# Attention and GEGLU in one kernel: the q, k, v products as pairs of half-depth matmuls

## The chip, the cores and the metric

One Trainium2 chip, of which one core is used. The metric is the time of one execution in device microseconds (us), from runs on the chip; lower is better. The core's engines are TensorE (PE in the profile, its weight loads PEld), VectorE (DVE), ScalarE (ACT), GpSimd (POOL), and SyncE (SP), which here issues all transfers. Each takes its instructions in a fixed order. Matmul results go to PSUM, eight banks of 128 partitions x 512 float32, from where VectorE or ScalarE must fetch them.

## The reference

```python
def _A_ref(x, wqkv, wo):
    ...
    qkv = (lambda x, *d: x.transpose(*d))((x @ wqkv).reshape(B, S, 3, H, Dh), 2, 0, 3, 1, 4)
    q, k, v = qkv[0], qkv[1], qkv[2]
    scores = jnp.einsum("bhqd,bhkd->bhqk", q, k) * (Dh ** -0.5)
    p = _softmax(scores, axis=-1)
    o = jnp.einsum("bhqk,bhkd->bhqd", p, v)
    return (lambda x, *d: x.transpose(*d))(o, 0, 2, 1, 3).reshape(B, S, D) @ wo

def _B_ref(x, w_gate, w_up, w_down):
    return (_gelu(x @ w_gate) * (x @ w_up)) @ w_down

xn = _layernorm(x, axis=-1)
s = _A_ref(xn, A_wqkv, A_wo)
g = _silu(_B_ref(xn, B_w_gate, B_w_up, B_w_down))
return x + s * g
```

Here S = 2048 tokens, D = 576, 32 heads of 18, F = 4608; all float32. The change concerns `x @ wqkv` alone.

## The kernel before

The kernel has a first stage (the `pro` pool, up to line 384), in which x is normalised and transposed and q, k, v are computed and stored to DRAM; a long second stage, in which sections of the feed-forward part (gate, up, down) run interleaved with attention; and an epilogue. Everything that changes lies in the first stage.

**Precision.** A float32 operand is cut into a high part, rounded by the copy into an fp32r tile, and a low part, the difference. A product is the sum of high x high, low x high and high x low.

**Depth.** D = 576 is four tiles of 128 rows (KT = 4) and 64 rows over (HR = 64). A product's list `TERMS` has 12 full terms and two for the 64 rows over: there the x tile `xtr` holds the high part in partitions 0 to 63 and the low part in 64 to 127, and the weights' 64 rows are loaded twice, so that one matmul does both. That is 14 matmuls of 128 rows. `mm_terms` (L174) issues them into one PSUM tile `po`.

**Blocks.** Tokens are taken in four blocks of 512 (loop at L351). For each block nine q/k products (`project`, L286), each 128 columns of wqkv by 512 tokens, in the order 4, 5, 0, 1, 6, 7, 8, 2, 3; then `store_xt` (L245) stores the transposed x; then the 20 transposes of the next block (`transposes`, L234, five PSUM tiles `pt`, split into high and low parts by `split_t`, L185); then eight v products (`values_of`, L294), each 128 tokens by 288 columns. TensorE's order is the order of the program text; on the other engines a scheduler places each instruction, and SP's queue too.

**Evictions.** A q/k product is copied by ScalarE into a high part (L290), VectorE subtracts to the low part (L291), and both parts are stored (L293). The two tiles have three buffers each, so the fourth product waits for the first one's stores. A v product is copied by ScalarE (L300) into one of eight `vn` tiles and stored (L301).

**The next block's x.** `load_x` (L194) loads four tiles of 128 tokens (`xx`, four buffers, free again when the transposes of the block before have read them). `norm` (L203) takes statistics of each tile on VectorE (`bn_stats` L209, two per tile, `bn_aggr` L213), a square root on ScalarE (L215), small steps (L218 to L221), and normalises the four tiles (L223); ScalarE copies each tile's last 64 columns (L225). All of it is called in one piece after the fifth q/k product (n == 4, L370).

**Weights.** In block 0 the weights are loaded into five buffers `rawp` (L171) as they come free. The q/k weights are split on GpSimd (L106, L108), the v weights on ScalarE and VectorE (L116, L117). Eight small stores of zeros (L376) go to a DRAM tile `zq`.

**PSUM in this stage.** Three banks `po` and five banks `pt`.

Of the kernel before, what the change touches and what calls it, by code (L numbers as in the profile page):

```python
# [8 lines left out]
F32 = mybir.dt.float32  # L9
F32R = mybir.dt.float32r  # L10
AF = mybir.ActivationFunctionType
ALU = mybir.AluOpType
# [5 lines left out]
P = 128  # L18
NT = S // P
TB = 512  # L20
NB = S // TB
KT = 4
# [32 lines left out]
def f(ap):  # L55
    return ap.bitcast(F32)
# [13 lines left out]
def kernel(ctx: ExitStack, tc: tile.TileContext, x, wqkv, wo, w_gate, w_up, w_down, out):  # L70
# [65 lines left out]
    def load_xd(b, key=None):  # L136
# [13 lines left out]

    TERMS = [(0, k, 0) for k in range(KT)] + [(1, k, 0) for k in range(KT)] + [(0, k, 1) for k in range(KT)] \
        + [(0, KT, 2), (1, KT, 2)]

    FIRST_TERMS = sorted(TERMS[:2 * KT], key=lambda t: 2 * t[1] + 3 * t[0]) + TERMS[2 * KT:]


    with tc.tile_pool(name="pro", bufs=1) as pro, tc.tile_pool(name="pps", bufs=1, space=PSUM) as pps:
# [15 lines left out]

        def mm_terms(o, w, cols, xt, toks, swap=False, terms=TERMS):  # L174

            for i, (wp, k, xp) in enumerate(terms):
                xx = xt[xp][:, k, toks] if xp < 2 else xt[2][:, toks]
                ww = w[wp][:, k, cols] if k < KT else w[2 + wp]
                st, m = (xx, ww) if swap else (ww, xx)
                nc.tensor.matmul(o, st, m, start=(i == 0), stop=(i == len(terms) - 1))  # L180

        def tmp2(name):
            return pro.tile([P, TB], F32R, name=name, tag=name, bufs=3)

        def split_t(pt, k, xt):  # L185
# [16 lines left out]

        def norm(xr, b, between=None, behind=None):  # L203
            keep = tc.keep_in_program_order if b == 1 else lambda i: i
            st = pro.tile([P, 4, 8], F32, name="st", bufs=2)
            for j in range(4):
                bs = pro.tile([P, 2, 6], F32, name="bs", bufs=2)
                for h in range(2):
                    one = nc.vector.bn_stats(bs[:, h, :], xr[j][:, 288 * h:288 * h + 288])  # L209
                    keep(one)  # L210
                if behind and j == 0:
                    behind(one)
                nc.vector.bn_aggr(st[:, j, 0:2], bs)  # L213
            var, r, t = st[:, :, 1], st[:, :, 3], st[:, :, 4]
            nc.scalar.activation(t, var, AF.Sqrt, bias=eps)  # L215
# [12 lines left out]
        def warm(n):  # L228

            o = pps.tile([P, TB], F32, name="po", bufs=3)  # L230
# [21 lines left out]
        XT = [(pro.tile([P, KT, TB], F32R, name=f"xth{i}"), pro.tile([P, KT, TB], F32R, name=f"xtl{i}"),  # L252
               pro.tile([P, TB], F32R, name=f"xtr{i}")) for i in range(2)]
        VN = [pro.tile([P, H // 2, DH + 1], F32, name=f"vn{i}") for i in range(8)]
        eps = pro.tile([P, 1], F32, name="eps")
# [30 lines left out]
        def project(b, t, xt):  # L286
            o = pps.tile([P, TB], F32, name="po", bufs=3)
            mm_terms(o, WQK[t], slice(0, P), xt, all_t, terms=FIRST_TERMS if b == 0 and t == ORDER[0] else TERMS)
            hi, lo = tmp2("t1"), tmp2("t2")
            nc.scalar.activation(hi, o, AF.Copy)  # L290
            nc.vector.tensor_tensor(lo, o, f(hi), op=ALU.subtract)  # L291
            for i, a in enumerate((hi, lo)):
                nc.sync.dma_start(qk[i, t * P:(t + 1) * P, b * TB:(b + 1) * TB], f(a))  # L293

        def values_of(b, j, c, xt):
            t = b * 4 + j
            o = pps.tile([P, TB], F32, name="po", bufs=3)
            mm_terms(o[:, 0:D // 2], WV[c], slice(0, D // 2), xt, slice(j * P, (j + 1) * P), True)
            v = VN[2 * j + c]
            nc.scalar.activation(v[:, :, 1:DH + 1], o[:, 0:D // 2].rearrange("p (h d) -> p h d", d=DH), AF.Copy)  # L300
            nc.sync.dma_start(vs[t * P:(t + 1) * P, c * H // 2:(c + 1) * H // 2, :], v)  # L301

# [32 lines left out]
        xr = load_x(0)  # L335
        last = norm(xr, 0, first_hi, first_loads)
        raw, (raw_r, rest) = ahead_qk.pop(0)[1], ahead_qk.pop(1)
# [9 lines left out]
        for b in range(NB):  # L347
            for n, t in enumerate(ORDER):
# [693 lines left out]
```

## Time and profile before

| | us |
|---|---|
| median of 3 runs | 2547.48 (2546.96 to 2547.53) |
| profiled execution: span from first to last instruction | 2545.4 |
| first q/k matmul to first gate matmul | 11.68 to 196.27 |

The time of the profiled execution itself is not given apart from its span; the median of the runs is 2.1 us above that span. A row of a timeline is: start in us, length in us, engine, line, operation, tile written, tiles read, shape, count, and in brackets the idle time before it with what ended it. A row of groups is: line, engine, operation, tiles, shapes, count, then busy us, mean ns of one, and idle time before with what ended most of it. A row of the chain of waits has start, length, engine, tile and line. SPq is SP issuing a transfer; the transfer lands later.

### The profile page before, as it was taken

The page shows a single profiled execution, that of the slowest core. Times are in us where ns is not written, and L with a number is a line of the kernel's source. Part 1 is how long each engine was busy: PE and PEld are TensorE (multiplying, and loading weights), DVE is VectorE, ACT ScalarE, POOL GpSimd, SP SyncE. Part 2 cuts the span into 40 slices and gives each one's busy share as a digit, 9 for nine tenths or more (in the row PEclk, how much of TensorE's full clock was granted, in tenths as well). Part 3 has the DMA queues.
Part 4 walks back from the last instruction along what each step waited for, and adds up shares of the span by engine and source line. Part 5 has one row for each costly group of instructions (what it writes and reads, how often), then busy time and mean ns, then how long its engine had stood idle before and what let it go on. Part 6 is the DMA issues. An engine that isn't in the chain of part 4 may idle for free.

```text
span 2545.4 us, 63167 instructions
## 1 busy us (share of the span) xinstructions
PE 2538.4 (100%) x23974; PEld 2008.4 (79%) x23974; DVE 1950.4 (77%) x3499; ACT 1555.1 (61%) x3050; POOL 1320.7 (52%) x1447
## 2 busy tenths in 40 slices
PE   9999999999999999999999999999999999999999
PEld 8888877777777777777777787777777777787798
DVE  5316988888888888888888888888888888887277
ACT  3223366666677666676666677666676666676612
POOL 2117545555465554445565545554446555455675
PEclk9999999999999999999999999999999999999999
DMA  8876444444465444444455444444446444444483
GB/s 267 269 241 158 100 103 106 100 111 109 107 150 121 104 109 112 113 112 110 111 125 140 116 111 106 105 108 112 109 109 153 115 109 109 108 106 99 114 242 107
DMA packets 398686, 325.51 MB, mean 128 GB/s; under 512 B 117408, under 2 KB 309184, under 8 KB 398384
## 3 DMA queue, kind: packets, MB, share of 16 engines
q1 hardware_dynamic: 398384, 321.47, 49.7%
q8 instruction: 191, 3.13, 0.5%
q14 instruction: 111, 0.91, 0.1%
HBM read 266.63 MB, written 54.70 MB: 126 GB/s over the span
## 4 chain that ended last, share of the span: by engine, by line
PE 98%; ACT 1%; DVE 0%; DMA 0%; SPq 0%; issue 0%; ACTq 0%
PE pg L413 29%; PE py L465 18%; PE acc L764 18%; PE pm L698 9%; PE pe L729 9%; PE po L180 7%; PE pu L413 6%; PE po L902 2%; ACT pT L730 1%; PE pt L241 0%; SPq L665 0%; DMA xx<-in_A_x_dram 0%; DVE bs L209 0%; ACT t L426 0%; DMA KS<-qk 0%
## 5 line engine op out<-in xcount | busy, mean ns | idle before, releaser
L730 ACT ACTIVATE pT<-pe 128x512 f32<-128x512 f32 x2048 | 1153.3, 598 | 368.7 <-PE pm L698 226.3
L699 DVE TENSOR_REDUCE mx<-pm 128x1 f32<-128x512 f32 x2048 | 1249.6, 680 | 151.3 <-PE pm L698 149.0
L413 PE MATMUL pg<-xd,wh 64*128 64x512 f32 x2592 | 928.9, 390 | 0.0
L413 PE MATMUL pu<-xd,wh 64*128 64x512 f32 x2592 | 928.6, 390 | 0.0
L698 PE MATMUL pm<-KS,q 64*128 64x512 f32 x2048 | 779.0, 388 | 0.8 <-DMA KS<-qk 0.5
L729 PE MATMUL pe<-q,KS 64*128 64x512 f32 x2048 | 775.2, 387 | 0.0
L413 PEld LDWEIGHTS pg<-xd,wh 64*128 64x128 f32 x2592 | 476.5, 184 | 115.9 <-POOL wh L106 21.1
L413 PE MATMUL pg<-xd,wl 64*128 64x512 f32 x1296 | 501.6, 387 | 0.0
L413 PE MATMUL pu<-xd,wl 64*128 64x512 f32 x1296 | 501.4, 387 | 0.0
L413 PEld LDWEIGHTS pu<-xd,wh 64*128 64x128 f32 x2592 | 477.0, 184 | 2.0
L764 PE MATMUL acc<-pT,VS 128*32 128x512 f32 x4096 | 452.8, 594 | 0.0
L108 POOL TENSOR_TENSOR wl<-raw,wh 128x384 fp32r<-128x384 f32 x432 | 434.2, 1019 | 13.7
L106 POOL TENSOR_SCALAR hh<-t 128x512 fp32r<-128x512 f32 x128 | 79.1, 618 | 652.0 <-DVE t L440 637.8
L698 PEld LDWEIGHTS pm<-KS,q 64*128 64x128 f32 x2048 | 374.2, 184 | 31.1 <-DVE mx L699 4.3
L729 PEld LDWEIGHTS pe<-q,KS 64*128 64x128 f32 x2048 | 370.9, 184 | 21.9
L465 PE MATMUL py<-dh,hh 64*128 64x288 f32 (+1 forms) x2160 | 360.3, 294 | 0.3
L465 PE MATMUL py<-dl,hh 64*128 64x288 f32 (+1 forms) x2160 | 358.7, 292 | 0.0
L465 PE MATMUL py<-dh,hl 64*128 64x288 f32 (+1 forms) x2160 | 358.3, 292 | 0.0
L764 PEld LDWEIGHTS acc<-pT,VS 128*32 128x32 f32 x4096 | 127.4, 110 | 289.9 <-issue 278.0
L106 POOL TENSOR_SCALAR wh<-raw 128x384 fp32r<-128x384 f32 x432 | 217.2, 515 | 143.7 <-PE pu L413 83.4
L453 DVE TENSOR_TENSOR Y<-py,Y 128x288 f32<-128x288 f32 x544 | 227.1, 452 | 59.8 <-PE py L465 52.7
L413 PEld LDWEIGHTS pg<-xd,wl 64*128 64x128 f32 x1296 | 238.7, 184 | 32.1
(119 smaller groups left out, 3106.7 us busy)
## 6 DMA issues: line engine op xcount, KB each, us to landing
KS<-qk SPq DMA_DIRECT2D x1536, 36.0 KB
raw<-in_B_w_gate_dram SPq DMA_DIRECT2D x144, 288.0 KB
raw<-in_B_w_up_dram SPq DMA_DIRECT2D x144, 288.0 KB
raw<-in_B_w_down_dram SPq DMA_DIRECT2D x67, 576.0 KB
VS<-vs SPq DMA_DIRECT2D x128, 152.0 KB
qk<-t SPq DMA_DIRECT2D x72, 256.0 KB
q<-qk SPq DMA_DIRECT2D x384, 36.0 KB
xx<-in_A_x_dram SPq DMA_DIRECT2D x32, 288.0 KB
```

Source lines behind the costliest of these rows:

```text
L106: first = nc.gpsimd.tensor_scalar(hi, raw, 1.0, 1.0, op0=ALU.mult, op1=ALU.mult)
L108: low_part[:] = [keep(nc.gpsimd.tensor_tensor(lo, raw, f(hi), op=ALU.subtract))]
L180: nc.tensor.matmul(o, st, m, start=(i == 0), stop=(i == len(terms) - 1))
L413: nc.tensor.matmul(o, w[1 + wp][k][rr, c, :], xd[xp][k][rr, c, :], start=(i == 0), stop=(i == len(terms) - 1))
L453: one = kept(nc.vector.tensor_tensor(yy, py, yy, op=ALU.add))
L465: return nc.tensor.matmul(py, hs[g][a][rr, j * P:(j + 1) * P], wd[w][rr, g, 288 * c:288 * c + 288], start=start, stop=stop)
L698: nc.tensor.matmul(pm, QS[u, r][rr, t * P:(t + 1) * P], KS[(u * NA + c) % KB][r][rr, :], start=True, stop=True)
L699: nc.vector.tensor_reduce(MX[u][:, 2 * r + a, t, c:c + 1], pm, axis=AX.X, op=ALU.max)
L729: nc.tensor.matmul(pe, KS[(u * NA + c) % KB][r][rr, t * P:(t + 1) * P], QS[u, r][rr, :], start=True, stop=True)
L730: nc.scalar.activation(PT[u, kt][:, 2 * r + a, :], pe, AF.Exp, scale=SCALE)
L764: nc.tensor.matmul(ACC[u][32 * a:32 * a + 32, :], VS[(u * NA + c) % VB][:, v:v + 32], pt[:, a, :], start=first, stop=last, skip_group_chec ...
L902: nc.tensor.matmul(po, parts_of(b, j)[x_][:, k, :], OW[w][c][k], start=(i == 0), stop=(i == len(OUT) - 1))
```

## The change

Every product is now done in two halves of 64 rows, one in partitions 0 to 63, one in 64 to 127, each with its own PSUM tile; their matmuls are issued alternately. `REST` gives the halves the terms of the 64 rows over: one half gets two of the three, the other one, and which is which changes from product to product, so that a product has 27 halves. Where one half has one more, it waits in the list `HALVES` and is paired with the next product's first. A second x tile `xtq` holds the 64 rows with the high and low parts the other way round.

The two sums are added when a product is fetched: for q and k, ScalarE copies the first sum into the low part's tile, VectorE adds the second to it, ScalarE makes the high part, VectorE the low part; for v, ScalarE copies and VectorE adds. All PSUM tiles of the stage, the transposes' too, come from one pool of eight banks. `vn` has five tiles instead of eight. `norm` is cut in two functions: statistics of tiles 0 and 1 after one product, of tiles 2 and 3 after the next, and the rest after the one behind that (after products 5, 6 and 7 in block 0, after 3, 4 and 5 in later blocks).

```diff
-    TERMS = [(0, k, 0) for k in range(KT)] + [(1, k, 0) for k in range(KT)] + [(0, k, 1) for k in range(KT)] \
-        + [(0, KT, 2), (1, KT, 2)]
+    TERMS = [(0, k, 0) for k in range(KT)] + [(1, k, 0) for k in range(KT)] + [(0, k, 1) for k in range(KT)]
...
+    REST = [[[(0, KT, 2), (1, KT, 2)], [(0, KT, 2)]], [[(0, KT, 3)], [(0, KT, 3), (1, KT, 3)]]]
...
-        def mm_terms(o, w, cols, xt, toks, swap=False, terms=TERMS):
...
+        HALVES = [[], []]
+        PRODUCTS = [0]
+
+        def product(shape, operands, put, terms=TERMS):
+
+            pos = [pps.tile([P, TB], F32, name="po", bufs=8)[:, 0:shape] for _ in range(2)]
+            parity = PRODUCTS[0] % 2
+            PRODUCTS[0] += 1
+            left = [0]
+            for a in range(2):
+                mine = terms + REST[parity][a]
+                left[0] += len(mine)
+                for i, term in enumerate(mine):
+                    def step(a=a, i=i, term=term, n=len(mine)):
+                        st, m = operands(slice(HR * a, HR * a + HR), *term)
+                        nc.tensor.matmul(pos[a], st, m, start=(i == 0), stop=(i == n - 1))
+                        left[0] -= 1
+                        if left[0] == 0:
+                            put(*pos)
+                    HALVES[a].append(step)
+            while all(HALVES):
+                for half in HALVES:
+                    half.pop(0)()
...
-                nc.scalar.activation(xt[2], pt, AF.Copy)
-                nc.vector.tensor_tensor(xt[2][HR:P, :], pt[HR:P], f(xt[2])[HR:P, :], op=ALU.subtract)
+                for i, (hi, lo) in enumerate((HALF, HALF[::-1])):
+                    nc.scalar.activation(xt[2 + i], pt, AF.Copy)
+                    nc.vector.tensor_tensor(xt[2 + i][lo, :], pt[lo], f(xt[2 + i])[lo, :], op=ALU.subtract)
...
-            pts = [pps.tile([P, TB], F32, name="pt", bufs=KT + 1) for k in range(KT + 1)]
+            pts = [pps.tile([P, TB], F32, name="po", bufs=8) for k in range(KT + 1)]
...
-        VN = [pro.tile([P, H // 2, DH + 1], F32, name=f"vn{i}") for i in range(8)]
+        VN = [pro.tile([P, H // 2, DH + 1], F32, name=f"vn{i}") for i in range(5)]
...
+            def put(o, o2):
+                hi, lo = tmp2("t1"), tmp2("t2")
+                both = f(lo)
+                nc.scalar.activation(both, o, AF.Copy)
+                nc.vector.tensor_tensor(both, both, o2, op=ALU.add)
+                nc.scalar.activation(hi, both, AF.Copy)
+                nc.vector.tensor_tensor(lo, both, f(hi), op=ALU.subtract)
+                for i, a in enumerate((hi, lo)):
+                    nc.sync.dma_start(qk[i, t * P:(t + 1) * P, b * TB:(b + 1) * TB], f(a))
...
+            def put(o, o2):
+                vv = v[:, :, 1:DH + 1]
+                nc.scalar.activation(vv, o.rearrange("p (h d) -> p h d", d=DH), AF.Copy)
+                nc.vector.tensor_tensor(vv, vv, o2.rearrange("p (h d) -> p h d", d=DH), op=ALU.add)
+                nc.sync.dma_start(vs[t * P:(t + 1) * P, c * H // 2:(c + 1) * H // 2, :], v)
...
-                if n == 4 and b + 1 < NB:
-                    norm(xr, b + 1)
+                early = 0 if b == 0 else 2
+                if n in (4 - early, 5 - early) and b + 1 < NB:
+                    if n == 4 - early:
+                        st = pro.tile([P, 4, 8], F32, name="st", bufs=2)
+                    h = n - 4 + early
+                    norm_stats(xr, b + 1, st, range(2 * h, 2 * h + 2))
+                if n == 6 - early and b + 1 < NB:
+                    norm_rest(xr, st)
...
+        last_steps()
```

More of the change, by code (lines that the diff above doesn't have):

```diff
@@ L172, in load_rows, with last_steps, x_part, w_part @@
             return raw
-        def mm_terms(o, w, cols, xt, toks, swap=False, terms=TERMS):
[L176 to L180, printed above, removed]
+        HALVES = [[], []]
[19 more added lines that the diff above has]
+                    half.pop(0)()
+        def last_steps():
+            for half in HALVES:
+                while half:
+                    half.pop(0)()
+        def x_part(xt, rr, k, xp, toks):
+            return xt[xp][rr, k, toks] if xp < 2 else xt[xp][rr, toks]
+        def w_part(w, rr, k, wp, cols):
+            return w[wp][rr, k, cols] if k < KT else w[2 + wp][rr]
         def tmp2(name):
             return pro.tile([P, TB], F32R, name=name, tag=name, bufs=3)
+        HALF = slice(0, HR), slice(HR, P)
         def split_t(pt, k, xt):
@@ L201, in load_x, with norm_stats @@
             return xr
-        def norm(xr, b, between=None, behind=None):
+        def norm_stats(xr, b, st, js, behind=None):
             keep = tc.keep_in_program_order if b == 1 else lambda i: i
-            st = pro.tile([P, 4, 8], F32, name="st", bufs=2)
-            for j in range(4):
+            for j in js:
                 bs = pro.tile([P, 2, 6], F32, name="bs", bufs=2)
@@ L252 @@
         XT = [(pro.tile([P, KT, TB], F32R, name=f"xth{i}"), pro.tile([P, KT, TB], F32R, name=f"xtl{i}"),
[L253 to L254 removed]
+               pro.tile([P, TB], F32R, name=f"xtr{i}"), pro.tile([P, TB], F32R, name=f"xtq{i}")) for i in range(2)]
+        VN = [pro.tile([P, H // 2, DH + 1], F32, name=f"vn{i}") for i in range(5)]
         eps = pro.tile([P, 1], F32, name="eps")
@@ L335 @@
         xr = load_x(0)
-        last = norm(xr, 0, first_hi, first_loads)
+        st = pro.tile([P, 4, 8], F32, name="st", bufs=2)
+        norm_stats(xr, 0, st, range(4), first_loads)
+        last = norm_rest(xr, st, first_hi)
         raw, (raw_r, rest) = ahead_qk.pop(0)[1], ahead_qk.pop(1)
```

23 lines of the change are left out of this document (10 added, 13 removed).

## The prediction

> **What bounds the kernel now.** I read the page first, then the chain of waits in order of time, then the engines one by one over the first 100 us.
>
> ```profile
> span 2545.4 us, 63167 instructions
> PE 2538.4 (100%) x23974; PEld 2008.4 (79%) x23974; DVE 1950.4 (77%) x3499; ACT 1555.1 (61%) x3050; POOL 1320.7 (52%) x1447
> PE 98%; ACT 1%; DVE 0%; DMA 0%; SPq 0%; issue 0%; ACTq 0%
> ```
>
> TensorE ends the chain for 98% of the span, so time taken off it counts in full, and so does every wait put in front of it. In order of time, the part that changes is this:
>
> ```profile
> 11.68 30.17 PE po L180 x126
> 41.85 2.18 PE pt L241 x20
> 44.04 44.32 PE po L180 x238
> 137.04 59.23 PE po L180 x350
> 196.27 0.43 PE pg L413
> ```
>
> From 11.68 to 196.27 us TensorE never pauses: nine q/k products (126 = 9 x 14 matmuls), 20 transposes, eight v products and the nine of the next block (238 = 17 x 14), and so on. I call the products of a block P0 to P8 and v0 to v7. After 196.27 us the order of instructions is the same in both programs on every engine, so what is won or lost by then stays to the end.
>
> **The matmuls: what the pairs save.**
>
> ```profile
> 18.82 1.09 PE L180 MATMUL po<-xth,qh 128*128 128x512 f32 x4
> 22.09 1.09 PE L180 MATMUL po<-xth,qh 128*128 128x512 f32 x4
> 205.67 0.39 PE L413 MATMUL pg<-xd,wh 64*128 64x512 f32 x1
> 207.71 0.39 PE L413 MATMUL pg<-xd,wh 64*128 64x512 f32 x1
> 444.36 6.36 PE py L465 x95
> L465 PE MATMUL py<-dh,hh x32: 285/290/297, 444.2 to 450.2; 64*128 64x288 f32 x32
> ```
>
> One q/k product of 14 full matmuls takes 22.09 - 18.82 = 3.27 us (233.6 ns each). The gate and up products are already such pairs of halves: nine of them in 207.71 - 205.67 = 2.04 us, 226.7 ns a pair. The new product has 27 halves, 13.5 pairs: 3.06 us. 36 products save 36 x 0.21 = 7.6 us. A v product takes (44.32 - 9 x 3.27)/8 = 1.86 us, 132.9 ns a matmul; the down products' 48 pairs of 288 columns (three groups of 32 halves) take 6.36 us, 132.5 ns a pair, so 13.5 pairs take 1.79 us, and 32 products save 2.3 us. Together **-9.9 us**, and v gains only by the half pair that is gone.
>
> ```profile
> 238.11 0.39 PE L413 MATMUL pu<-xd,wh 64*128 64x512 f32 x1
> 238.43 0.40 PE L465 MATMUL py<-dh,hh 128*128 128x288 f32 x1
> 241.66 0.29 PE L465 MATMUL py<-dh,hl 128*128 128x288 f32 x1
> 241.88 0.50 PE L413 MATMUL pg<-xd,wh 64*128 64x512 f32 x1
> 242.22 0.39 PE L413 MATMUL pg<-xd,wl 64*128 64x512 f32 x1
> ```
>
> Going from pairs to full matmuls costs 0.32 - 0.23 = 0.09 us, the way back (0.22 - 0.13) + (0.34 - 0.23) = 0.2 us. The change goes out for transposes three times and back four times and loses the one switch at 196.27; without the two that fall into the pause of block 0 below that is **+0.6 us**. [...] If each of the five were a whole matmul record of 0.39 us, the sum would be 2.0 instead of 0.6 us; the rows above show less.
>
> **The evictions: what the sum costs.**
>
> ```profile
> L290 ACT ACTIVATE t<-po 128x512 fp32r<-128x512 f32 x36 | 21.4, 596 | 77.8 <-PE po L180 65.3 <-DMA qk<-t 9.6 <-issue 2.5
> L291 DVE TENSOR_TENSOR t<-po,t 128x512 fp32r<-128x512 f32 x36 | 24.9, 691 | 86.0 <-ACT t L290 76.7 <-DMA qk<-t 6.7 <-DMA raw<-in_A_wo_dram 2.6
> L437 ACT ACTIVATE t<-t 128x512 f32<-128x512 f32 x4 | 2.5, 632 | 1.2 <-DVE t L427 1.2
> L300 ACT ACTIVATE vn<-po 128x288 f32<-128x288 f32 x32 | 13.2, 418 | 40.0 <-PE po L180 40.0
> L209 DVE BATCH_NORM_STATS2 bs<-xx 128x6 f32<-128x288 f32 x32 | 12.8, 441 | 18.1 <-DMA xx<-in_A_x_dram 18.0
> L453 DVE TENSOR_TENSOR Y<-py,Y 128x288 f32<-128x288 f32 x544 | 227.1, 452 | 59.8 <-PE py L465 52.7
> ```
>
> A q/k product was two operations, 0.60 + 0.69; now it is copy, add, high part, low part: 0.60 + 0.69 + 0.63 (the nearest copy from SBUF is L437's) + 0.69 = 2.6 us one after the other. For the new SBUF-only subtraction the rows give 0.69 to 1.0 us (L117 below); I take 0.69. Within a q/k stage this is 1.4 us of VectorE per 3.06 us of TensorE and hidden: the eight banks hold four products. A v product was one copy on ScalarE; now it also needs an add on VectorE (0.45 us, L453's), **behind whatever VectorE has in its queue**, and there stand the next block's statistics, which waited 18 us for x without harm to anyone. The transposes' five banks, separate before, now come out of the same eight. The third copy of the remaining x rows (0.63 on ScalarE, 0.69 on VectorE per block) is in the chains below; three fewer fills of the v tiles gain nothing, as VectorE waits for x then anyway.
>
> ```profile
> 20.24 3.62 SPq L376 DMA_DIRECT2D zq<-ident  x8
> 23.96 1.82 SPq L293 DMA_DIRECT2D qk<-t  x4
> 32.56 1.15 SPq L171 DMA_DIRECT2D rawp<-in_A_wqkv_dram  x2
> 46.66 0.42 SPq L249 DMA_DIRECT2D xhs<-xth  x1
> 55.63 0.90 SPq L199 DMA_DIRECT2D xx<-in_A_x_dram  x2
> 20.37 2.53 POOL L108 TENSOR_TENSOR ql<-rawp,qh 128x512 fp32r<-128x512 f32 x2
> 26.41 0.60 ACT L290 ACTIVATE t<-po 128x512 fp32r<-128x512 f32 x1 [3.52 <-DMA qk<-t]
> 40.39 0.69 ACT L116 ACTIVATE vh<-rawp 128x576 fp32r<-128x576 f32 x1 [1.35 <-DMA rawp<-in_A_wqkv_dram]
> 40.98 0.24 ACT L225 ACTIVATE xx<-xx 128x64 f32<-128x64 f32 x1
> 28.14 1.01 DVE L117 TENSOR_TENSOR rest<-raw,rest 128x576 fp32r<-128x576 f32 x1
> 41.99 1.42 DVE L117 TENSOR_TENSOR vl<-rawp,vh 128x576 fp32r<-128x576 f32 x2
> 38.02 0.21 DVE L213 BATCH_NORM_AGGREGATE st<-bs 128x2 f32<-128x12 f32 x1
> 39.42 2.05 DVE L223 TENSOR_SCALAR xx<-xx,st 128x576 f32<-128x576 f32 x4
> 58.88 0.82 DVE L209 BATCH_NORM_STATS2 bs<-xx 128x6 f32<-128x288 f32 x2 [9.50 <-DMA xx<-in_A_x_dram]
> ```
>
> **Block 0, up to the transposes.** In the changed program's order SP has two v weight loads (the x2 at 32.56) ahead of the eight small stores (20.24) and the first q/k store. The second of them needs a buffer that GpSimd frees with its fifth low part, about 22.9 (20.37 + 2.53). So the first store goes at 22.9 + 0.5 + 3.6 = 27.1 instead of 23.96. P3's copy waits for P0's low part to be stored: that is the second store, 27.6, and 2.45 us to land (23.96 to 26.41) gives 30.0. From there ScalarE and VectorE run in one chain: P3 to 32.6, a weight split to 33.5, two tiles' statistics (2 x 1.03) to 35.6, P4's and P5's add, high and low parts to 39.6, the other two tiles' statistics to 41.7, square root and small steps (38.23 to 39.42, 1.2) to 42.9, first normalised tile at 43.4. TensorE arrives at 11.68 + 30.17 - 9 x 0.21 = 40.0. Then it needs five of the eight banks: two that P5 used, free by then, both of P6's, and the first of P7's. P7's copy stands on ScalarE behind the last normalised tile (44.9), that tile's 0.24 copy, two v weight splits (1.4), P6's high part (0.63) and itself takes 0.60: free at 47.8. Sixteen transposes (1.7) end at 49.5, where without waits it would be 42.15: **+7.4 us**. Bounds: 0, if stores and evictions run as early as before, and 10, with each SBUF subtraction at 1.0 us and the stores a microsecond later.
>
> **Block 0, v products.** v0 needs the first bank that the transposes fill. ScalarE first ends P7's high part and the last two v weight splits (1.4), then copies that bank (0.60), VectorE subtracts (0.69): free at 52.6, 3.1 us late. Before v0's add VectorE has seven more operations of 0.69 (three splits, two for the remaining rows, P8's add and low part), so it ends at 57.9; then come the statistics of block 2. Their x loads stand behind 2.36 MB of stores of transposed x. Before, from the first of these (46.66) to the first x in place (58.88) 3.43 MB took 12.2 us, 281 GB/s; now 2.65 MB from about 50.8 give 60.3, then one tile every 1.05 us, the fourth (issued behind v0's store) near 65. VectorE's order is three tiles, v1's add (64.0), the fourth tile, root, v2's add (67.2), four normalisations, v3's add (70.6). v5, v6 and v7 need the banks of v1, v2 and v3: v5 starts at 64.0, v6 at 67.2, v7 at 70.6 and ends at 72.4. From 49.5 that is 22.9 us against 8 x 1.79 = 14.3: **+8.6 us**. Bounds: 3.1, if x is there in time, and 13, if x comes at 200 GB/s.
>
> **Blocks 1 and 2.** In block 1, x loads stand ahead of the big stores. VectorE after the transposes (time T): five splits, one tile, a split, v0's add T+6.6, three tiles, v1's add T+9.8, root and normalisation, v2's add T+13.5. v5 waits 0.8, v6 1.9 us, v7 ends at T+17.1: **+2.8 us** (bounds 0 and 5.5, block 0's waits for x). At the end of block 2 no statistics are left, but P8's last half stands behind the transposes and its bank is freed by 0.60 + 0.69 us: **+1.1 us** (0 to 1.3).
>
> The sum: -9.9 + 0.6 + 7.4 + 8.6 + 2.8 + 1.1 = +10.6 us. On the span of 2545.4 that is 2556.0; the median of the runs, 2547.48, lies 2.1 above the span, so **2558.1 us**.
>
> **Rivals.** (a) The gain alone: SP's queue keeps pace, so stores and x land early enough for the eight banks to cover the rest. 2547.5 - 9.9 + 0.6 = 2538.2. For it:
>
> ```profile
> 50.00:75.00 25.00, 25.00 (x138) 21.86 (x137) 9.61 (x24) 5.53 (x15) 0.00 (x0) 1.00 0.94 322
> ```
>
> In the 25 us from 50 on VectorE (the third busy time) works only 9.6 and ScalarE 5.5 us, so there is room for 3.6 us of adds. Against it: each engine takes its instructions in a fixed order, L209's 18 us of waits stand in VectorE's, and the DMA engines are 0.94 busy here. It decides once the first q/k store goes out by 24 and x of block 2 is in place by 57.9. (b) One of the two pauses of block 0 is hidden: without the 7.4, +3.2, 2550.7. For it: before, the same stage just made it, with x normalised at 41.47 (39.42 + 2.05) and the transposes starting at 41.85. (c) More waiting: x at 200 GB/s (the 13 instead of 8.6) and slow subtractions (the 10 instead of 7.4), +7.0 on top, 2565.1. For it: L117 on 576 columns took 1.01 us at 28.14 while GpSimd still worked on its splits, and 0.71 (1.42 for two) at 41.99. (d) The change doesn't do what it says and the halves run one after the other: 36 x 13.5 x 0.227 + 32 x 13.5 x 0.1325 = +168 us; against it speaks that nine pairs of 512 columns took 2.04 us above, and each half's record alone is 0.39 us. 2715.
>
> **How the numbers follow.** Forecast 0.62 (its own range 2552 to 2564), (a) 0.10, (b) 0.12, (c) 0.14, (d) 0.02. The range 2546 to 2568 takes in the forecast, (b) and (c). 0.2% is 5.1 us, about what a measurement of this kernel tells from no change. Slower: forecast, (c), (d) and a fourth of (b), 0.81; same: the rest of (b), 0.09; faster: (a), 0.10.
>
> **What would show it.** In the profile after: a q/k product every 3.06 us in blocks 1 to 3; the transposes of block 1 starting near 43 and ending near 49.5, waiting for x and then for banks; the v products of block 0 taking about 23 us with TensorE waiting for VectorE's adds, and L209 waiting for x ahead of them; gate and up starting near 207. It would be wrong if VectorE's adds never stand behind a statistics instruction that waits, or if the first q/k store goes out before 24.

## The result, and the profile after

The changed kernel took 2563.42 us (median of 5 runs, 2561.81 to 2564.84), the kernel before 2547.48 us (5 runs, 2546.96 to 2547.57): 1.0062 times as long, 95% interval 1.0051 to 1.0073, 15.9 us slower. The forecast was 2558.1 us, with a range of 2546 to 2568. The profiled execution took 2561.81 us, its span is 2560.0, 14.6 more than the span before.

The page of the changed kernel, its first line, its busy times, and the chain by engine:

```profile
span 2560.0 us, 65090 instructions
PE 2539.7 (99%) x24858; PEld 2018.4 (79%) x24858; DVE 1993.1 (78%) x3568; ACT 1578.9 (62%) x3090; POOL 1326.0 (52%) x1447
PE 94%; DMA 1%; DVE 1%; ACT 1%; SPq 1%; POOL 1%; issue 0%; ACTq 0%; POOLq 0%
```

TensorE had 98% of the chain; now it has 94, and the rest is a string of short waits for DMA, VectorE, ScalarE and queues. The order of time shows where. The table gives the start of the first matmul or transpose of each stage, read from TensorE's timeline (us from the start of the span; the chain of waits gives some starts up to 0.35 us later).

| stage starts | before | after | later by |
|---|---|---|---|
| q/k products, block 0 | 11.68 | 13.71 | 2.03 |
| transposes of block 1 | 41.69 | 46.01 | 4.32 |
| v products, block 0 | 43.79 | 53.43 | 9.64 |
| q/k products, block 1 | 58.80 | 74.94 | 16.14 |
| v products, block 1 | 90.30 | 105.93 | 15.63 |
| q/k products, block 2 | 105.30 | 121.68 | 16.38 |
| v products, block 2 | 136.79 | 152.56 | 15.77 |
| q/k products, block 3 | 151.80 | 167.95 | 16.15 |
| v products, block 3 | 181.19 | 196.42 | 15.23 |
| gate and up | 196.20 | 210.80 | 14.60 |

Nearly all is lost by the end of block 0's v products; the q/k products after that, without the transposes behind them, win back 0.75, 0.84 and 0.92 us (28.65, 28.55 and 28.47 us against 29.39). The end of the span is 14.6 us later too.

Timeline of block 0 in the changed kernel, four engines one below the other. Columns: start, duration (us), engine, line; in brackets the engine's idle time before it and what ended it. Dots stand for rows left out.

```profile
28.30 1.83 SPq L332 DMA_DIRECT2D qk<-t  x4
...
32.37 0.60 ACT L327 ACTIVATE t<-po 128x512 f32<-128x512 f32 x1 [5.85 <-DMA qk<-t]
...
44.13 0.30 ACT L248 ACTIVATE st<-st,eps 128x4 f32<-128x4 f32 x1 [2.66 <-DVE st L244]
...
46.01 1.16 PE L274 MATMUL po<-ident,xx 128*128 128x128 f32 x3 [3.36 <-DVE xx L256]
47.98 0.47 PE L274 MATMUL po<-ident,xx 128*128 128x128 f32 x1 [0.82 <-DVE t L328]
49.82 3.68 PE L274 MATMUL po<-ident,xx 128*128 128x128 f32 x16 [1.36 <-ACT t L327]
...
63.55 1.19 DVE L240 BATCH_NORM_STATS2 bs<-xx 128x6 f32<-128x288 f32 x3 [4.37 <-DMA xx<-in_A_x_dram]
...
66.12 0.40 DVE L346 TENSOR_TENSOR vn<-vn,po 128x288 f32<-128x288 f32 x1
...
66.57 0.67 PE L191 MATMUL po<-vh,xth 64*128 64x288 f32 x6 [2.52 <-DVE vn L346]
...
69.11 1.28 PE L191 MATMUL po<-vh,xth 64*128 64x288 f32 x8 [0.54 <-ACT vn L345]
...
72.62 1.28 PE L191 MATMUL po<-vh,xth 64*128 64x288 f32 x8 [1.02 <-ACT vn L345]
```

Read downwards, it is the chain that the prediction wrote out, each step somewhat later. The first q/k store goes at 28.3 instead of 23.96; the fourth product's copy waits 5.85 us for a stored t tile; ScalarE's square root waits for the second piece of the statistics; TensorE waits for normalised x and then twice for banks that q/k evictions hold. In the v products a statistics instruction waits 4.37 us for x, the v add stands behind it, and TensorE waits for the add.

What the chain does not show is the clock. Busy time of each engine in five stretches of the changed kernel; the number after the five engines is the granted TensorE clock, then DMA share and GB/s:

```profile
8.00:10.90 2.90, 0.84 (x8) 0.84 (x9) 2.37 (x8) 1.33 (x4) 0.00 (x0) 1.00 0.97 216
10.90:14.40 3.50, 3.50 (x19) 3.06 (x19) 1.38 (x4) 1.95 (x5) 2.79 (x5) 0.51 0.88 234
14.40:45.00 30.60, 28.25 (x242) 27.36 (x238) 19.17 (x35) 10.57 (x20) 16.01 (x15) 1.00 0.69 206
45.00:55.40 10.40, 7.17 (x32) 5.38 (x34) 9.33 (x18) 8.04 (x18) 0.00 (x0) 0.51 0.55 192
55.40:75.00 19.60, 15.33 (x211) 14.20 (x211) 12.17 (x32) 5.10 (x15) 0.00 (x0) 1.00 0.95 329
```

With two pauses, of 2.13 us (up to 10.06) and of 3.36 us (up to 46.01), TensorE went to half clock (0.51 in the table); with the pause of 2.52 us up to 66.57 it did not (1.00). At half clock sixteen transposes took 3.68 us (at 49.82); before, at a granted clock of 1.00, all twenty took 2.18.

The gain itself, first matmuls of q/k and v products of block 3, where nothing waits:

```profile
171.12 1.18 PE L191 MATMUL po<-xth,qh 64*128 64x512 f32 x8
177.44 1.19 PE L191 MATMUL po<-xth,qh 64*128 64x512 f32 x8
196.42 0.78 PE L191 MATMUL po<-vh,xth 64*128 64x288 f32 x8
198.24 0.73 PE L191 MATMUL po<-vh,xth 64*128 64x288 f32 x8
```

The two q/k rows are two products apart: 3.16 us for one, not the 3.06 of the prediction. Divided by 13.5 pairs that is 234 ns a pair, as long as a full matmul before. A v product takes 1.82 us (forecast 1.79).

### The profile page after: what moved, and what is told of

It is laid out like the page before. It is cut to its first block, busy times and chain, and to the rows that moved or that the text cites. A ratio compares the mean times of both kernels' runs of the same rounds, so it can differ in the third digit from the quotient of the medians.

```text
span 2560.0 us, 65090 instructions
## 1 busy us (share of the span) xinstructions
PE 2539.7 (99%) x24858; PEld 2018.4 (79%) x24858; DVE 1993.1 (78%) x3568; ACT 1578.9 (62%) x3090; POOL 1326.0 (52%) x1447
## 4 chain that ended last, share of the span: by engine, by line
PE 94%; DMA 1%; DVE 1%; ACT 1%; SPq 1%; POOL 1%; issue 0%; ACTq 0%; POOLq 0%
PE pg L470 29%; PE py L522 18%; PE acc L821 18%; PE pm L755 9%; PE pe L786 9%; PE pu L470 5%; PE po L191 5%; PE po L959 2%; ACT pT L787 1%; DMA xx<-in_A_x_dram 1%; DMA qk<-t 0%; DMA xhs<-xtl 0%; SPq L722 0%; DVE xx L256 0%; POOL ql L108 0%
```

## The experiments

The theory to be tested: two separate losses in block 0, (1) the transposes of block 1 behind late evictions, (2) v adds on VectorE behind statistics that wait for x. Durations of stages are again differences of first starts.

**v_whole: the v products alone undone.**

```diff
...
-            product(D // 2, operands, put)
+            o = whole(D // 2, operands)
+            nc.scalar.activation(v[:, :, 1:DH + 1], o.rearrange("p (h d) -> p h d", d=DH), AF.Copy)
+            nc.sync.dma_start(vs[t * P:(t + 1) * P, c * H // 2:(c + 1) * H // 2, :], v)
...
+            last_steps()
             store_xt(b, xt)
```

(`whole` issues the 14 matmuls of 128 rows into one bank. With `last_steps` the q/k half that is left over at the end of a block no longer waits over the transposes. Every kernel below that uses `whole` has this line.)

> The v products go back to 14 matmuls of 128 rows in one bank with ScalarE's copy alone; the q/k products stay pairs. Theory (VectorE's adds of the v products stand behind statistics that wait for x, and the banks come free late): the v products of block 0 take 14.5 to 15.0 us instead of 21.5, those of block 1 about 14.9 instead of 15.8, and the time falls by some 7 to 9 us to 2554 to 2556, with the pause ahead of block 1's transposes (4.4 us of waiting, v starting near 53) unchanged. Rival (the banks of the v products are late because of the q/k products' evictions ahead of them, which stay): block 0's v products keep 19 us or more, and the time stays above 2560.

2557.37 us (2556.38 to 2557.93), 1.0038 [1.0024, 1.0052]. TensorE's timeline at block 1's transposes:

```profile
46.44 0.41 PE L282 MATMUL po<-ident,xx 128*128 128x128 f32 x2 [3.83 <-DVE xx L264]
```

And the v products in the chain of waits:

```profile
53.93 15.32 PE po L210 x112
```

112 matmuls, eight products, stand there in one piece. The stage took 15.6 us instead of 21.5, the pause ahead of it stayed. Statistics still waited for x here (7.6 us, for block 2), but TensorE did not. So loss (2) belongs to the v pairs; whether to their adds or to their second bank, adds_first shows below. The time fell by 6.1 us, a little less than expected: the v products took more than the 14.5 to 15.0 us expected, and TensorE waited 0.8 us for q/k evictions at the transposes of block 2.

**qk_whole: the q/k products alone undone**, with their two-step eviction.

```diff
-                both = f(lo)
-                nc.scalar.activation(both, o, AF.Copy)
-                nc.vector.tensor_tensor(both, both, o2, op=ALU.add)
-                nc.scalar.activation(hi, both, AF.Copy)
-                nc.vector.tensor_tensor(lo, both, f(hi), op=ALU.subtract)
...
+            o = whole(TB, operands, FIRST_TERMS if b == 0 and t == ORDER[0] else TERMS)
+            hi, lo = tmp2("t1"), tmp2("t2")
+            nc.scalar.activation(hi, o, AF.Copy)
+            nc.vector.tensor_tensor(lo, o, f(hi), op=ALU.subtract)
```

> The q/k products go back to 14 matmuls of 128 rows with the two-step eviction; the v products stay pairs with the add. Theory (the four-step evictions of q/k, kept late by the first q/k store at 28.3 us, hold block 1's transposes): the first q/k store goes near 25, v of block 0 starts near 46 to 47 instead of 53.4 (the start stays 2.0 us late), v of block 0 still takes about 21 us, the q/k product goes from 3.17 to 3.27 us, and the time is 2563.4 - 8 + 36 x 0.1 = about 2559. Rival (the two-piece statistics and their place make the transposes late): v of block 0 still starts near 53 and the time is near 2567.

2558.04 us (2557.11 to 2558.68), 1.0040 [1.0025, 1.0055]. From its timeline, SyncE's queue and TensorE:

```profile
23.85 1.83 SPq L337 DMA_DIRECT2D qk<-t  x4
...
42.65 2.34 PE L282 MATMUL po<-ident,xx 128*128 128x128 f32 x20
44.93 0.80 PE L191 MATMUL po<-vh,xth 64*128 64x288 f32 x8
...
63.53 1.33 PE L191 MATMUL po<-vh,xth 64*128 64x288 f32 x7 [4.55 <-DVE vn L349]
```

Twenty transposes in one run, as before, and v starts 32.4 us after the first product (before 32.1, changed kernel 39.7). The v products took 22.1 us with their wait for the add. So the losses belong to different halves of the change, (1) to q/k and (2) to v; the pieces of the statistics, which are still in this kernel, are not (1) by themselves. Undoing each half alone gave 6.1 and 5.4 us of the 15.9. Where the other 4.4 us come from was not separated: from the two together, or from what both kernels still have (five vn tiles, one pool of banks, the third copy of x).

**adds_first: the v pairs kept, statistics behind the adds.**

```diff
                     keep(one)
+                    if ADDS:
+                        no_sync(one, ADDS[-1], "adds first")
```

(`ADDS` collects the v adds, `no_sync` fixes the order on VectorE.)

> The changed kernel as it is, but the statistics of block 2 (and 3) are put behind the last v add of block 0 (and 1) on VectorE. Theory (adds behind statistics that wait for x): block 0's v products take 14.4 to 15 us, no wait of TensorE for the vn add there, and the time falls by 7 to 9 us to about 2554 to 2556. Rival (ScalarE's copies and the add's own time keep the banks, wherever the statistics stand): 19 us or more, and 2560 or more.

2557.36 us (2556.66 to 2558.66), 1.0038 [1.0023, 1.0053]. Block 0's v products took 15.2 us and TensorE did not wait for an add there: the theory held in its place, and since each v product keeps its two banks and its add here, loss (2) is the add's place behind the statistics. The time stayed above the expected 2556 because the wait partly moved on, into block 1's q/k products. Timeline of ScalarE, VectorE and TensorE:

```profile
69.96 0.41 ACT L347 ACTIVATE vn<-po 128x288 f32<-128x288 f32 x1 [5.15 <-DMA vs<-vn]
...
79.77 3.86 DVE L258 TENSOR_SCALAR xx<-xx,st 128x576 f32<-128x576 f32 x3
...
84.28 1.19 PE L191 MATMUL po<-xth,qh 64*128 64x512 f32 x7 [1.75 <-DVE t L330]
```

And the busy times of the stretch after it, with the granted clock:

```profile
85.50:88.90 3.40, 3.40 (x18) 2.64 (x16) 2.49 (x4) 1.86 (x4) 2.87 (x2) 0.50 0.76 238
```

With five vn tiles instead of eight, ScalarE's copy waits for a vn tile's store; the adds end late, then the statistics, and the q/k evictions of block 1 behind them: a pause of 1.75 us, and 3.4 us of half clock after it. That stage took 32 us, where the changed kernel needs 28.6.

**store_first: the queue's order.** The v weight loads now stand behind the first product's two stores, and the small zq stores behind the first of them.

```diff
+                no_sync(i, store, "store first")
+                tc.keep_in_program_order(i)
...
+                    no_sync(nc.sync.dma_start(zq[:, i * HR:(i + 1) * HR], ident[0:HR - MROW, HR:P]), STORES[0], "store first")
```

> The changed kernel as it is, but SyncE's queue issues the first q/k stores ahead of the two v-weight loads and the first one ahead of the eight zq stores. Theory (the first store at 28.3 us keeps the three t buffers, and with them the evictions and the banks of block 1's transposes): the first store goes at 20 to 22 us, the third copy of a q/k product starts near 26 instead of 32.4, v of block 0 starts 3 to 6 us before 53.4, and the time is 2557 to 2560. Rival (four steps for each eviction on ScalarE and VectorE are too slow in block 0, whose weights these engines also split, wherever the stores stand): v still starts within 1 us of 53.4 and the time stays near 2563. If the pause ahead of the transposes shrinks under 2 us, the 10.2 us of half clock after it should go too.

2560.55 us (2559.63 to 2561.36), 1.0050 [1.0035, 1.0065]. Timeline of SyncE's queue, ScalarE and TensorE:

```profile
20.61 1.48 SPq L336 DMA_DIRECT2D qk<-t  x2
...
25.77 0.58 ACT L331 ACTIVATE t<-po 128x512 f32<-128x512 f32 x1
...
31.29 0.60 ACT L331 ACTIVATE t<-po 128x512 f32<-128x512 f32 x1 [2.57 <-DMA qk<-t]
...
42.64 0.41 PE L274 MATMUL po<-ident,xx 128*128 128x128 f32 x2 [1.70 <-DVE xx L256]
44.62 0.33 PE L274 MATMUL po<-ident,xx 128*128 128x128 f32 x1 [0.96 <-DVE t L332]
46.46 3.58 PE L274 MATMUL po<-ident,xx 128*128 128x128 f32 x16 [1.51 <-ACT t L331]
```

The fourth product's copy, which the expectation calls the third, came at 25.77, as expected, but the fifth waited for the next store, and the stretch from the first transpose to v stayed at 7.3 us (changed kernel 7.4). v started 38.1 us after the first product instead of 39.7: the queue's order is worth about 1.7 us here, not the whole 7.4 that the prediction hung on it. The pause was down to 1.70 us, with two shorter ones behind it, and half clock followed all the same (sixteen transposes took 3.58 us), though for 3.4 us instead of 10.2; the 2 us of the expectation were an estimate that no run bears out. The median fell by 2.9 us, but the span of the profiled execution by only 0.4: it lost 2.6 us after the first gate matmul, where a pause of 1.32 us (228.75 to 230.07) was followed by 3.4 us of half clock (granted clock 0.66 over 230 to 235).

**qk_no_add: two eviction steps with pairs.** The second half's sum is left out.

```diff
-                both = f(lo)
-                nc.scalar.activation(both, o, AF.Copy)
-                nc.vector.tensor_tensor(both, both, o2, op=ALU.add)
-                nc.scalar.activation(hi, both, AF.Copy)
-                nc.vector.tensor_tensor(lo, both, f(hi), op=ALU.subtract)
+                nc.scalar.activation(hi, o, AF.Copy)
+                nc.vector.tensor_tensor(lo, o, f(hi), op=ALU.subtract)
```

> The changed kernel, but a q/k product's second half is computed and then left out: the eviction has two steps again (ScalarE's copy of the first half into the high part, VectorE's subtraction), so the output lacks those halves. Theory (the two further steps of each eviction make block 1's transposes late): TensorE waits less than 2 us in all from its last q/k product of block 0 to the first v product, v starts near 47, and the time falls by 6 us to about 2557. Rival (the steps are not it: two banks for each product, evicted behind the statistics, the normalisation and the v-weight split, make the passage whatever an eviction's steps are): the passage from first transpose to v keeps 6 us or more and the time stays above 2560.

2559.51 us (2558.84 to 2560.31), 1.0044 [1.0030, 1.0057]. Timeline of ScalarE and TensorE:

```profile
31.48 0.60 ACT L326 ACTIVATE t<-po 128x512 fp32r<-128x512 f32 x1 [8.65 <-DMA qk<-t]
...
44.92 0.88 PE L274 MATMUL po<-ident,xx 128*128 128x128 f32 x3 [2.84 <-DVE xx L256]
49.22 3.89 PE L274 MATMUL po<-ident,xx 128*128 128x128 f32 x17 [3.43 <-DVE t L327]
```

The rival held for the passage: it took 8.1 us with evictions of two steps, as in the kernel before (the time came out half a microsecond under the rival's 2560). The stores are late here too, and TensorE waits for VectorE's last subtractions, which stand behind statistics, normalisation and the split of the v weights. Fewer steps alone don't help while stores are late, and earlier stores alone don't while the steps are four. Both together, and the two banks for each product by themselves, were not tried.

**one_piece: the third part of the change undone.** Statistics and normalisation in one piece after the fifth product.

```diff
-                if n in (4 - early, 5 - early) and b + 1 < NB:
...
+                if n == (4 if b == 0 else 4) and b + 1 < NB:
+                    st = pro.tile([P, 4, 8], F32, name="st", bufs=2)
+                    norm_stats(xr, b + 1, st, range(4))
+                    norm_rest(xr, st)
```

> The changed kernel with the next block's statistics and normalisation in one piece after the fifth product, as before the change. Theory (the second piece stands late on VectorE, ScalarE's square root waits 2.7 us for it, and the last evictions stand behind that): TensorE's wait ahead of block 1's transposes falls from 3.4 to under 1 us, v of block 0 starts 2 to 3 us earlier and the time is 2560 to 2561. Rival (the evictions of the last products are the limit, the pieces only say where the wait stands): the transposes start earlier but last longer, v of block 0 starts within 1 us of the changed kernel's 39.7 us after the first product, and the time stays at 2562 to 2564.

2562.90 us (2561.29 to 2563.36), 1.0056 [1.0042, 1.0070]. TensorE's timeline:

```profile
40.77 1.58 PE L191 MATMUL po<-xth,qh 64*128 64x512 f32 x7 [2.75 <-DVE t L328]
...
49.53 3.68 PE L274 MATMUL po<-ident,xx 128*128 128x128 f32 x16 [0.67 <-ACT t L327]
```

Most of the pause moved from the transposes into the q/k products ahead of them, and v started 41.2 us after the first product, 1.5 later than in the changed kernel. The waits from there to v are 2.75 + 1.36 + 0.70 + 0.67 = 5.5 us; in the changed kernel they are 3.36 + 0.82 + 1.36, also 5.5. So the rival's reading holds, that the pieces decide where the wait stands and not how long it is, and so does its time. Two of its marks do not: the transposes start later than in the changed kernel (33.6 us after the first product, not 32.3), and v not within 1 us of 39.7.

**memsets_8: the start.** The changed kernel's first product came at 13.71, 2.0 us late, with the first stretch of half clock. Three further memsets put back what VectorE did there before.

```diff
-        for v in VN:
+        for v in VN + VN[:3]:
             nc.vector.memset(v, 1.0)
```

> The changed kernel with three more memsets of the vn tiles on VectorE at the start, eight as before the change. Theory (with three memsets fewer the statistics, and with them the first weight loads, go 0.2 us earlier and collide with x): the first product starts near 11.7 us instead of 13.7, without a drop of the granted clock near 11 us, and the time falls by 2.0 us to about 2561.4. Rival (when the fourth x tile lands is chance: with the same five memsets the other runs started at 11.9 to 12.7): the start lies anywhere between 11.7 and 13.7 and the time between 2561 and 2563.5.

2563.88 us (2560.80 to 2564.38), 1.0061 [1.0047, 1.0074]: no difference. The first product came at 11.93, but so it did, at 11.91 to 12.85, in the other seven kernels with five memsets; the twenty transposes ahead of it took 2.40 us in six of them and 2.77 in weights_shifted, against 3.72 in the changed kernel. So the 2.0 us do not come from the memsets alone; each of these kernels was profiled once, and what moves the start was not found. What this run gained there it lost at block 1's v products, by TensorE's timeline:

```profile
117.47 1.29 PE L191 MATMUL po<-vh,xth 64*128 64x288 f32 x8 [1.44 <-ACT vn L345]
```

and by the busy times around that row:

```profile
113.00:119.00 6.00, 4.47 (x61) 4.02 (x59) 5.32 (x17) 2.46 (x9) 0.00 (x0) 1.00 0.80 287
119.20:122.50 3.30, 3.30 (x32) 3.30 (x30) 0.45 (x1) 0.41 (x1) 0.00 (x0) 0.50 0.56 158
```

A pause of 1.44 us was followed by half clock; the same place of the changed kernel, with 0.63 us, had none (granted clock 1.00).

**weights_shifted: why a pair takes 234 ns.**

```diff
+        pad1 = pro.tile([P, 8], F32, name="pad1")
+        nc.gpsimd.memset(pad1, 0.0)
         VN = [pro.tile([P, H // 2, DH + 1], F32, name=f"vn{i}") for i in range(5)]
```

> The changed kernel with a tile of 32 bytes put ahead of the vn tiles, so that the q/k weights lie 32 bytes further: weights and x then have the same place within 64 bytes, as weights and x of the gate and up products have. Theory (a pair takes 234 ns instead of 227 because the two operands lie differently): the pair falls to 227 ns, a q/k product of block 3 from 3.16 to 3.07 us, and the time by 36 x 0.09 = 3.3 us to about 2560. Rival (the 7 ns don't come from where the operands lie): 234 ns and 2563.

2565.56 us (2563.78 to 2568.19), 1.0071 [1.0057, 1.0084]. Two q/k products of block 3, two products apart:

```profile
172.47 1.18 PE L191 MATMUL po<-xth,qh 64*128 64x512 f32 x8
178.71 1.17 PE L191 MATMUL po<-xth,qh 64*128 64x512 f32 x8
```

A product takes 3.12 us by these two rows. Over all q/k products of block 3 the mean pair takes 232.1 ns against 234.0, so 1.9 of the 7 ns follow where the tiles lie. The time is no better, for the waits in blocks 0 and 1 were longer in this run (v of block 1 took 18.7 us instead of 15.8: behind a pause of 1.48 us four pairs took 0.96 us, at 123.60, where they took 0.53 at 57.70). Where the other 5 ns come from is open.

**Can a part of it pay?** Three kernels kept pairs only where less waits. v_pairs_only joins the edits of qk_whole, adds_first and memsets_8.

> q/k products of 14 matmuls of 128 rows as before, v products as pairs, the statistics behind the v adds of the block before, eight memsets. Theory (the loss is adds behind statistics and q/k evictions ahead of transposes; without both, the pairs of v keep their gain): no pause over 1 us in blocks 0 and 1, v of block 0 near 14.5 to 15 us, and a time of 2547.5 - 4 x 0.5 = about 2545.5, up to 2547.5. Rival (the vn tiles, five instead of eight, make ScalarE's copies wait for the stores behind the xhs stores whatever VectorE does): v of block 0 takes 16 us or more, or the statistics come late for block 2's transposes, and the time is 2549 or more.

2549.77 us (2548.76 to 2551.56), 1.0008 [0.9999, 1.0018]. From the chain of waits, block 1's v products and block 2's q/k products:

```profile
92.10 14.60 PE po L191 x216
106.70 29.69 PE po L210 x126
```

No pause of over 0.4 us from the first product to the end of the last v product, no half clock (mean granted clock 1.000), and no gain. Eight v products of block 1 in pairs took 14.60 us (before 15.0), but by stage starts the transposes ahead of them took 2.27 (before 2.11) and the nine q/k products behind them 29.59 (before 29.39). So most of the 0.4 us that the pairs won went into the two changes between whole matmuls and pairs in each block; the rest went into the whole matmuls, which take 234.1 ns here and took 233.3 before. Block 0's v products took 15.95 us, with waits at the second product, so 16 us were not reached either. blocks_1_to_3 has block 0 whole and pairs from block 1 on, with adds_first and memsets_8.

```diff
-            product(D // 2, operands, put)
+            if b == 0:
+                o = whole(D // 2, operands)
...
+            else:
+                product(D // 2, operands, put)
```

(and the same in `project`.)

> Block 0 computes q, k and v as before the change, with 14 matmuls of 128 rows; blocks 1 to 3 in pairs; statistics behind the v adds of the block before, eight memsets. Theory (pairs pay by 0.1 us for a q/k product and 0.06 to 0.08 us for a v product, and the loss is all in block 0 and the stages it disturbs): 2547.5 - 27 x 0.1 - 24 x 0.07 = about 2543, faster than both kernels, with no pause over 1 us between 12 and 196 us. Rival (the four-step evictions make pauses at the transposes of blocks 1 and 2 too, or the first v adds still wait): 2547 to 2552.

2552.71 us (2549.08 to 2559.92), 1.0021 [1.0012, 1.0030]. Timeline of ScalarE and TensorE; the profiled execution is the longest of the eleven:

```profile
82.99 0.60 ACT L337 ACTIVATE t<-po 128x512 f32<-128x512 f32 x1 [3.57 <-DMA qk<-t]
...
92.66 0.33 PE L284 MATMUL po<-ident,xx 128*128 128x128 f32 x1 [3.18 <-ACT t L337]
94.53 3.68 PE L284 MATMUL po<-ident,xx 128*128 128x128 f32 x16 [0.68 <-ACT t L337]
```

The rival held: the same chain, copies waiting for t tiles' stores and transposes waiting for copies, now at the next transposes. The passage to v took 9.1 us there. Of the 12.7 us by which this span is longer than the one before, another 5.4 were lost after the first gate matmul: TensorE paused 2.31 us at 224.66 for a split of down weights on GpSimd, and 6.8 us of half clock followed (granted clock 0.52 over 226 to 233). Last, `b < 2` in the place of `b == 0`, with one_piece and memsets_8 and without adds_first, and the same with the 32 bytes of weights_shifted.

> Blocks 0 and 1 compute q, k and v as before the change, with 14 matmuls of 128 rows, blocks 2 and 3 in pairs; statistics in one piece, eight memsets, five vn tiles. Theory (a q/k product in pairs is worth 0.1 us and a v product 0.07 us wherever nothing waits, and stores and loads are less dense from block 2 on): 2547.5 - 18 x 0.1 - 16 x 0.07 = about 2544.5, faster than both kernels. Rival (pairs make a pause at block 3's transposes or at the first gate and up products, or five vn tiles do in blocks 0 and 1): 2546.5 to 2549.

> The same kernel with the 32 bytes ahead of the vn tiles that took the pair of a q/k product from 234.0 to 232.1 ns. Theory (the place of the operands is worth 1.9 ns a pair here too): 18 products of 13.5 pairs, 0.5 us less than the kernel without it, about 2544. Rival (the gain went into later waits, as the time of the whole kernel with the shift suggests): no difference, or slower.

2546.97 us (2544.98 to 2549.39), 0.9997 [0.9988, 1.0006], and 2547.26 us (2544.16 to 2548.34), 0.9994 [0.9985, 1.0003]. Neither can be told from the kernel before, nor from each other. The chain of the first has no wait left in it up to here:

```profile
90.98 14.92 PE po L210 x112
105.90 28.75 PE po L191 x242
134.65 2.33 PE po L282 x20
136.98 48.59 PE po L191 x532
```

In block 2, nine q/k products in pairs take 28.75 us against 29.39 and the v products 14.48 against 15.01, while the transposes between them take 2.33 instead of 2.10. In block 3 the q/k products take 28.33, but the v stage 15.45, with a pause of 0.39 us at its end. From the first q/k to the first gate matmul it is 183.25 us, and 182.66 with the shift, against 184.52 before. That is what the pairs are worth where hardly anything waits: 1.3 to 1.9 us for two blocks.

## Why the prediction was right, and where its sizes were off

Direction and mechanism held, and the size within the range: TensorE waits at both places that the text named, for the instructions that it named. That the sum came so near is in part luck: the steps below are off by -3.2 to +4.0 us and partly cancel, and the prediction's own narrower range, 2552 to 2564, held by 0.6 us. Step by step, measured by the stage starts:

| step | forecast, us | measured, us |
|---|---|---|
| start | 0 | +2.0 |
| 36 q/k products | -7.6 | -3.6 |
| from block 0's last q/k product to v | +7.4 | +8.7 |
| v stages, blocks 0 to 3, matmuls and waits | -2.3 + 8.6 + 2.8 + 1.1 = +10.2 | 6.5 + 0.75 + 0.4 - 0.6 = +7.0 |
| passages of blocks 1 and 2, switches between pairs and full matmuls | +0.6 | +0.5 |
| sum | +10.6 | +14.6 |

*q/k matmuls*: the term that was mis-sized. The price of a pair came from the gate and up products (226.7 ns); in the place of the q/k products a pair takes 234.0. The row of the full matmul there (233.6) was the nearer one, and it would have given 36 x (3.27 - 13.5 x 0.2336) = 4.2 us, which is what was found but for 0.6. The switches between pairs and full matmuls were sized right: +0.23 us at each of the passages of blocks 1 and 2. (Five whole records of 0.39 us, less the switch that is lost, would be 1.6 to 1.75 and not 2.0; either is more than was found.)

*Block 0 up to v*: the order of the chain was right, but its steps came 1 to 4 us later than worked out, and TensorE's own arrival too (42.65 instead of 40.0, of which 2.0 is the start). What the prediction did not have is the half clock: sixteen transposes took 3.68 us where 16/20 of 2.18, 1.7 us, were put down. Its weight on SyncE's order was too large: store_first gave back 1.7 us. Which part of the q/k half makes this loss, the four steps with late stores or the two banks for each product, stays open: qk_whole undoes all of it at once.

*Block 0's v products*: 21.5 us against 22.9, with the wait where it was put; v_whole and adds_first show that it is the add behind the statistics. That vn tiles, cut from eight to five, are a second limit behind it was not in the prediction; adds_first uncovered it, with copies that wait 5.15 us for a vn store; a kernel with pairs and eight tiles was not run. *Block 1*'s v products took 15.75 us against 17.1; why was not followed up.

*The rivals*: the gain alone (2538) falls, since the waits came, and even where the pairs run without one they bring 1 to 1.5 us a block, not 2.5. "More waiting" (2565.1) came nearest in the number, and its first part came in part: the first q/k store went 1.2 us later than forecast, and the first three SBUF subtractions took 0.98 to 1.00 us, the later ones 0.69. Its second part did not: from the first big store of x (53.04) to the first statistics (63.55) it took 10.5 us, where 9.5 were forecast and 200 GB/s would make 13. One pause hidden (2550.7) falls, as both came. That halves run one after the other falls with the 234 ns a pair.

The start's 2.0 us stand in the one profiled execution, which is the fastest of the five; whether the others had them too, and where they lost more, is not shown. That what is won or lost by the first gate matmul stays to the end held for the changed kernel (14.6 us at both places), but not for the profiled executions of store_first and blocks_1_to_3, which lost another 2.6 and 5.4 us behind it.

## What to carry to other kernels

Where TensorE never waited, fewer matmuls won little (1.3 to 1.9 us for two blocks), and with longer evictions the whole change lost 15.9 us: an added operation inherits the waits that stand ahead of it on its engine (the v add stood behind a statistics instruction's 4.37 us here), so list that queue, and the banks and buffers held meanwhile, before the edit. Take the price of a matmul from rows of the same stage and tiles, not from the same shape elsewhere (234.0 ns a pair here, 226.7 in the gate and up products). A pause of TensorE can cost more than its length (with the one of 3.36 us came 10.24 us of half clock), and taking one wait away may only show the next (a pause of 1.75 us in adds_first, of 2.75 in one_piece).

## What the runs showed of the hardware

The record of the granted clock has half clock (0.50) in the changed kernel from 10.96 to 14.37 us and from 45.09 to 55.33, 3.41 and 10.24 us long (the end of the span is left out here). Nine of the twelve experiments had some too, with a mean granted clock of 0.997 to 0.999; v_pairs_only, blocks_2_and_3 and blocks_2_and_3_shifted had 1.000. It came during or after pauses of 1.32 us (store_first, at 228.75; granted clock 0.66 over 230 to 235) to 4.73 us (weights_shifted, up to 47.65; sixteen transposes behind it took 3.45 us), but not with every one: behind a pause of 1.76 us at the start of qk_whole twenty transposes took 2.40 us (2.41 there in the kernel before, at 1.00), and behind the one of 2.52 us in the changed kernel the clock stayed at 1.00. What decides was not found. The kernel before ran at full clock from 5.5 to 2545.0 us, and its longest pause in that time was 0.52 us (at 301.7).

A pair of 64-row matmuls with 512 columns took 226.7 ns in the gate and up products, 234.0 in the q/k products, and 232.1 there with the weights 32 bytes further. Where the tiles lie is one part of it; the rest was not found. It is not the pairing: blocks_2_and_3 has both forms in one kernel, and there a whole matmul (block 1) and a pair (block 3) took 234.1 ns each, and with the shift 232.1 each, as means from start to start. So what the pairs save in the q/k products is the half matmul that a product has less, 13.5 in the place of 14.
